# A gated recurrence on one core: a new order of TensorE's work in its loop, and new places for three of its products in PSUM

## The chip, the cores and the metric

The kernel runs as one program on one core of a Trainium2 chip. The metric is the device time of an execution in microseconds (us). One more execution was taken by the hardware profiler; all rows below are from it. The engines are TensorE (PE in the rows, PEld for its weight loads), VectorE (DVE), ScalarE (ACT), GpSimd (POOL) and SyncE, which only issues DMAs (SP). Matrix products are written to PSUM, which has eight banks; PE writes there, DVE and ACT read there, and POOL does not.

## The reference, cut to what matters

```python
B, H, S, D = 4, 8, 768, 48
state = np.zeros((B, H, D, D))
for t in range(S):
    kt, vt, rt = k[:, :, t], v[:, :, t], r[:, :, t]
    cur = einsum('bhd,bhe->bhde', u[None] * kt, vt)          # the bonus
    y[:, :, t] = einsum('bhd,bhde->bhe', rt, state + cur)
    state = w[None, :, :, None] * state + einsum('bhd,bhe->bhde', kt, vt)
x = y as rows of tokens, 3072 x 384
x = moe(x)      # skip score, 8 experts, one for each token; w1 is 384 x 1024, w2 is 1024 x 384
return moe2(x)  # 32 soft slots, again 8 experts
```

The change touches the first part alone, the recurrence.

## The kernel before

The recurrence is cut into 24 tiles: tile j = 4c + b is chunk c (128 time steps, six chunks) of batch b, with all eight heads. The eight heads lie as four pairs, one head of a pair in partitions 0 to 47 and one in 64 to 111. Within a chunk the sum over earlier steps is a masked product, and across chunks the state is carried. For each tile the kernel does this:

- `prep` (DVE, lines 614 and 615): r and k times powers of the decay, into `rks`; on POOL the product `pd` = r times k (617), and `prepk` (POOL, 623) the keys `kt` scaled for the state.
- `scores` (PE): eight products `sc` of keys and queries (632), into two banks of their own, then four small products `dt` (635), the bonus of each step, into bank t. ACT copies `dt` to SBUF as `dts` (637).
- `upd` (PE, 654): eight products of `kt` and the values, the chunk's addition to the state, into columns 160 to 351 of the bank named ud; `moved` (ACT, 670) copies it to `us`. For tiles 20 to 23 there is no update.
- `bonus` (PE, 657): one transpose of `dts`, into columns 0 to 127 of the same bank ud, under the name `dtk`.
- `amask` (DVE): the scores times a mask (681, `past`), then a predicated copy that puts `dtk` on the diagonal (688). The result is `at`.
- `inter` (PE, 708): eight products of the state and `rs`, which open y's two banks; from chunk 1 on. In chunk 0 three warm-up products stand in its place (493).
- `av` (PE, 718): eight products of the values and `at`, added in y's banks; ACT copies them to `yt` (721).
- `trx` (PE, 727): four transposes of `yt`, into bank t; ACT copies them to `x` (728).
- `decayed` and `state` (POOL, 664 and 676): the state times the decay of a chunk, plus `us`.

Beside that the router of the first mixture of experts is worked off, a chunk at a time: `route1` (PE, 750, four products of 512 columns, copied by ACT at 751), `route2` (PE, 810, four transposes), `route2b` (DVE, 826 to 843), `route3` (PE, 853 to 862), `gates`, `places` and `count` (DVE, 867 to 894), `route4` (POOL 908, DVE 909), and `scat` (POOL, 897), an indirect DMA that sends the rows of one tile to their expert.

All five engines are scheduled by hand: each one works its instructions off in the order in which the program writes them. So the order of calls in the loop over i sets everything. Loop i of the recurrence does, on PE: `scores(i)`, `upd(i)`, `bonus(i)`, `route3` and `route1` where they fall, `inter(i-1)`, `trx(i-2)`, `av(i-1)`, and `route2`. From i = 5 on the router has a turn of four loops: `route1` and `route2` in the first (i = 6, 10, 14, 18), `route2b` in the second, `route3`, `gates`, `places` and `count` in the third, `route4` in the fourth. Waits between engines are placed by the framework, by the tiles that instructions share: who writes a PSUM tile waits until the others that use it are done with it. Bank t, bank ud and the pair of y exist once, and so does the pair of `sc`. `rks` has three buffers; `pd`, `kt`, `us`, `tmp`, `at` and `dts` have two.

After the loops comes a short stretch that ends the routing, and then the experts, some 200 us, with nothing of the recurrence in it. The weights of the first expert are loaded from loops 20 to 22 on (`wload`).

Of the kernel before, what the change touches and what calls it, by code (L numbers as in the profile page):

```python
# [8 lines left out]
F32 = mybir.dt.float32  # L9
# [10 lines left out]
P = 128  # L20
# [3 lines left out]
E = 8  # L24
# [442 lines left out]
def tile_main(ctx, tc, rk, kv, wu, wcat, phi, w1, w2, v1, v2, r_in, k_in, v_in, w_in, u_in, wcn, out, dbg=None, force=False):  # L467
# [157 lines left out]
    def scores(j):  # L625
        t = T[j]
        ks, rs = t["ks"], t["rs"]
        sc = t["sc"] = psc.tile([P, 2, 4, P], F32, tag="sc", name=f"sc{j}")
        for p in range(4):
            for hf in range(2):  # L630
                r0 = 64 * hf
                nc.tensor.matmul(sc[:, hf, p, :], ks[r0 : r0 + D, p, :], rs[r0 : r0 + D, p, :], start=True, stop=True)  # L632
        dt_ = ps.tile([P, P], F32, tag="t", name=f"dt{j}")
        for p in range(4):
            nc.tensor.matmul(dt_[32 * p : 32 * p + 32, :], usel[:, p, :], t["pd"][:, p, :], start=True, stop=True)
        t["dts"] = wk.tile([P, P], F32, tag="dts", name=f"dts{j}")
        nc.scalar.copy(t["dts"], dt_)

    def newud(j):
        t = T[j]  # L640
        t["ud"] = ps.tile([P, 352], F32, tag="ud", name=f"ud{j}")
        t["dk"] = t["ud"][:, 0 : P + 4 * E]
        t["dtk"] = t["ud"][:, 0:P]

    def upd(j):
        t = T[j]
        if j < NT - B:
            kt, kvt = t["kt"], t["kv"]
            up = t["up"] = t["ud"][0:PR, 160:352].rearrange("d (p e) -> d p e", p=4)
            for p in range(4):  # L650
                for g in range(2):
                    h = head(p, g)
                    m = 64 if g == 0 else D
                    nc.tensor.matmul(up[64 * g : 64 * g + m, p, :], kt[:, h * D : h * D + m], kvt[:, 1, h * D : h * D + D], start=True, stop=True)

    def bonus(j):
        nc.tensor.transpose(T[j]["dtk"], T[j]["dts"], ident)  # L657
# [8 lines left out]
    def moved(j):  # L666
        t = T[j]
        if j < NT - B:
            t["us"] = sp[j][1] if j < B else wk.tile([PR, 4, D], F32, tag="us", name=f"us{j}")
            nc.scalar.copy(t["us"], t["up"])  # L670

    def state(j):
        t = T[j]
        c, b = divmod(j, B)
        if 0 < c and j < NT - B:
            nc.gpsimd.tensor_add(sp[b][(c + 1) % 2], t["us"], t["tmp"])
# [46 lines left out]
    def trx(j, tag="t", pool=ps):  # L723
        c, b = divmod(j, B)
        trp = pool.tile([P, 4, P], F32, tag=tag, name=f"trp{j}")
        for p in range(4):
            nc.tensor.transpose(trp[:, p, 0:PR], yts[c][:, p, b, :], ident[:PR, :PR])
        nc.scalar.copy(
            x[:, j, 0:DM].rearrange("t (p f d) -> t p f d", p=4, f=2),
            trp.rearrange("t p (f d) -> t p f d", d=64)[:, :, :, 0:D],  # L730
        )
        del T[j]
# [241 lines left out]
    if True:  # L974
        for i in range(NT):
# [7 lines left out]
                    r0 = 64 * hf  # L983
                    nc.vector.tensor_copy(usel[r0 : r0 + D, :, hf : hf + 1], wt[r0 : r0 + D, 1, :].rearrange("p (a o) -> p a o", o=1))
            scores(i)
            newud(i)
            if i > 0:
                upd(i)
                moved(i)
            bonus(i)  # L990
            if rok and (rb == 3 or i == 23):
                route3(rc, place=T[i]["dk"][:, P:])
            if rok and rb == 1 and rc < 4:
                route1(rc)
            if i > 0:
                inter(i - 1)
            if i > 1:
                trx(i - 2)
            if i == 0:
                decays()  # L1000
                warm(ps, "y", 7)
                prep(1)
                prepk(0)
                prepk(1)
                for ts in spf:
                    for t in ts:
                        nc.gpsimd.memset(t[:, 4 * D :], 0.0)
                upd(0)
                moved(0)
            elif i + 1 < NT:  # L1010
                prep(i + 1)
                prepk(i + 1)
            if i == 22:
                route2(4)
                mrt = rows(nc, cn, "t", rt, pa, "u", mcs[:, 0:1])
            amask(i)
            if i == 22:
                nc.vector.tensor_copy(lx[:, 0:1, :], mrt)
            decayed(i)
            state(i)  # L1020
            if i > 0:
                av(i - 1)
            if i == 21:
                route4(3)
                route1(4)
                nc.vector.tensor_reduce(cmax, ltm[:, 0:16, :].rearrange("t b s -> t s b"), axis=AX.X, op=ALU.max)
                colmax(nc, cn, "t", pa, "u", mcs[:, 0:1], fourfold(nc, "t", rt, cmax))
            elif rb == 0 and 1 <= rc < 4:
                route4(rc - 1)
            if rok and rb == 1 and rc < 4:  # L1030
                route2(rc)
            if i == 22:
                route2b(4)
            if rok and rb == 2 and rc < 4:
                route2b(rc)
            if i == 23:
                route1(5)
# [9 lines left out]
            if rok and rb == 3:  # L1047
                weave("gpgpgp", g=gates(rc), p=places(rc))
                count(rc)
            if 20 <= i < 23:  # L1050
                wload(i - 20)
            if 2 <= i < 6:
# [500 lines left out]
```

## Time and profile before

| | us |
|---|---|
| median of 3 runs | 372.65 |
| lowest, highest | 371.74, 373.26 |
| the profiled execution | 372.8 |
| its span, first to last instruction | 370.6 |
| busy in the span: PE, DVE, ACT, POOL | 339.3, 246.9, 149.7, 122.6 |

The span is 2.2 us shorter than the profiled execution's own time. The recurrence's first score product starts 8.22 us into the span, and the last loop's at 135.58. A busy PE in these tables is modelled from when matmuls start, so the distance from one group's start to the next tells more than its busy time.

### The profile page before, as it was taken

How to read it: one execution, taken by the hardware profiler on the slowest of the kernel's cores; microseconds unless marked ns; L12 is line 12 of the kernel's file. 1: busy time of each engine (PE TensorE's matmuls, PEld its weight loads, DVE VectorE, ACT ScalarE, POOL GpSimd, SP SyncE). 2: the span in 40 equal slices, each digit the busy share in tenths (PEclk: the TensorE clock that was granted, in tenths of full speed). 3: DMA queues.
4: the chain of work that ended last, by engine and by line, in shares of the span. 5: the costliest groups of instructions: out<-in, count | busy, mean ns of one | idle time of the engine just before them, and what ended most of it. 6: DMA issues, size and time to landing. Idle time of an engine off the chain costs nothing. (4 is left out here: it accounts for less than half of the span.)

```text
span 370.6 us, 8677 instructions
## 1 busy us (share of the span) xinstructions
PE 339.3 (92%) x3473; PEld 269.9 (73%) x3473; DVE 246.9 (67%) x502; ACT 149.7 (40%) x319; POOL 122.6 (33%) x165
## 2 busy tenths in 40 slices
PE   8899988989889887999999999999999999999860
PEld 3566665766756566489999999999899999734350
DVE  5788588595877985766567574848566856426660
ACT  1233332433333223445464555554655553311270
POOL 3765567686885605420020211202020202020000
PEclk9999999999999998799999999999999999999995
DMA  7999956455564961199968788778876457849485
GB/s 207 247 276 331 286 176 186 126 196 156 168 204 134 356 221 44 50 308 330 321 234 292 263 255 287 258 235 261 301 249 210 138 206 217 297 154 399 178 312 205
DMA packets 45743, 85.93 MB, mean 232 GB/s; under 512 B 3625, under 2 KB 26495, under 8 KB 45696
## 3 DMA queue, kind: packets, MB, share of 16 engines
q1 hardware_dynamic: 42368, 79.87, 66.6%
q0 software_dynamic: 2800, 5.28, 4.6%
q8 instruction: 29, 0.48, 0.5%
q10 hardware_dynamic: 528, 0.16, 0.2%
q14 instruction: 18, 0.15, 0.1%
HBM read 74.51 MB, written 13.30 MB: 237 GB/s over the span
## 5 line engine op out<-in xcount | busy, mean ns | idle before, releaser
L1155 PE MATMUL hp<-xhl,wa 128*128 128x256 f32 x192 | 48.6, 290 | 0.2 <-ACT xhl L1145 0.2
L1156 PE MATMUL hp<-xhl,wa 128*128 128x256 f32 x192 | 47.2, 282 | 0.0
L1180 PE MATMUL yp<-wb,hh 128*128 128x384 f32 x128 | 45.3, 354 | 0.0
L955 DVE TENSOR_TENSOR wa<-w,wa 128x768 fp32r<-128x768 f32 x32 | 30.5, 954 | 22.1 <-ACT wa L967 22.1
L1213 POOL DMA_INDIRECT lt_d<-lsr,id x16 | 17.6, 1097 | 80.2 <-ACT xhl L1145 56.7
L1181 PE MATMUL yp<-wb,hh 128*128 128x384 f32 x128 | 43.1, 337 | 0.0
L1182 PE MATMUL yp<-wb,hlo 128*128 128x384 f32 x128 | 43.1, 337 | 0.0
L688 DVE COPY_PREDICATED at<-ident,ud 128x1024 f32<-128x1024 int32 x24 | 31.6, 1318 | 8.1 <-PE ud L657 5.4
L1155 PEld LDWEIGHTS hp<-xhl,wa 128*128 128x128 f32 x192 | 36.4, 189 | 0.5 <-ACT xhl L1145 0.5
L1156 PEld LDWEIGHTS hp<-xhl,wa 128*128 128x128 f32 x192 | 36.5, 190 | 0.0
L681 DVE TENSOR_TENSOR at<-sc,mask 128x1024 f32<-128x1024 f32 x24 | 29.3, 1219 | 10.2 <-PE sc L632 10.2
L617 POOL TENSOR_TENSOR pd<-rkb 112x512 f32<-112x512 f32 x24 | 30.8, 1284 | 9.4 <-DMA rkb<-in_rk_dram 6.8
L955 DVE TENSOR_TENSOR wb<-w,wb 128x768 fp32r<-128x768 f32 x32 | 30.5, 954 | 3.2 <-ACT wb L967 3.2
L897 POOL DMA_INDIRECT xs_d<-x,idx x24 | 24.3, 1011 | 21.2 <-DVE idx L883 10.2
L967 ACT CAST wb<-w 128x768 fp32r<-128x768 f32 x32 | 26.8, 838 | 9.0 <-PE yp L1182 5.1
L1166 DVE SCALAR_TENSOR_TENSOR hlo<-hp,hh 128x512 fp32r<-128x512 f32 x32 | 22.0, 688 | 12.4 <-ACT hh L1165 12.4
L1165 ACT ACTIVATE hh<-hp 128x512 fp32r<-128x512 f32 x32 | 19.1, 598 | 26.2 <-PE hp L1158 25.9
L1158 PE MATMUL hp<-xhl,wa 128*128 128x256 f32 x192 | 28.3, 283 | 0.0
L632 PE MATMUL sc<-rks 48*128 48x128 f32 x384 | 27.9, 285 | 0.0
L967 ACT CAST wa<-w 128x768 fp32r<-128x768 f32 x32 | 26.9, 840 | 0.0
L1180 PEld LDWEIGHTS yp<-wb,hh 128*128 128x128 f32 x128 | 24.1, 188 | 3.5 <-issue 3.5
L632 PEld LDWEIGHTS sc<-rks 48*128 48x128 f32 x384 | 23.3, 187 | 4.4 <-issue 2.3
(327 smaller groups left out, 663.2 us busy)
## 6 DMA issues: line engine op xcount, KB each, us to landing
w<-in_w_dram SPq DMA_DIRECT2D x32, 768.0 KB
v<-in_v_dram SPq DMA_DIRECT2D x29, 768.0 KB
rkb<-in_rk_dram SPq DMA_DIRECT2D x24, 448.0 KB
kvt<-in_kv_dram SPq DMA_DIRECT2D x24, 384.0 KB
out_dram<-ob SPq DMA_DIRECT2D x5, 768.0 KB
xs_d<-zt SPq DMA_DIRECT2D x4, 774.0 KB
xg<-xs_d POOLq DMA_DIRECT2D x6, 387.0 KB, 6.5
x<-in_v_dram SPq DMA_DIRECT2D x2, 768.0 KB
```

The source lines that it names most:

```text
L617: nc.gpsimd.tensor_mul(t["pd"], rkt[:, 0], rkt[:, 1])
L632: nc.tensor.matmul(sc[:, hf, p, :], ks[r0 : r0 + D, p, :], rs[r0 : r0 + D, p, :], start=True, stop=True)
L681: nc.vector.tensor_mul(at, t["sc"], mask.rearrange("s (a o t) -> s a o t", a=1, o=1).to_broadcast([P, 2, 4, P]))
L688: nc.vector.copy_predicated(at, ident_i.rearrange("s (a o t) -> s a o t", a=1, o=1).to_broadcast([P, 2, 4, P]), t["dtk"].rearrange("s (p o ...
L955: nc.vector.tensor_sub(lv, sl, hv.bitcast(F32))
L967: nc.scalar.copy(hv, sl)
L1155: nc.tensor.matmul(hp[:, f, :], hi[:, k, fs], xh[:, k, :], start=(k == 0 and f == 0), stop=False)
L1156: nc.tensor.matmul(hp[:, f, :], lo[:, k, fs], xh[:, k, :], start=False, stop=False)
L1158: nc.tensor.matmul(hp[:, f, :], hi[:, k, fs], xl[:, k, :], start=False, stop=(k == 2 and f == 1))
L1180: nc.tensor.matmul(YP[e][bl], hh[:, f, bs], hi[:, f, :], start=st, stop=False)
L1181: nc.tensor.matmul(YP[e][bl], hh[:, f, bs], lo[:, f, :], start=False, stop=False)
L1182: nc.tensor.matmul(YP[e][bl], hlo[:, f, bs], hi[:, f, :], start=False, stop=en)
```

## The change

The bonus products `dt`, their transpose `dtk` and the router's `rp` now lie in one bank, ud, in this order. The update of the state goes to columns 256 to 447 of the second of y's two banks, beside the sums of tile i-1; from the second chunk on it no longer carries the flag that starts an accumulation, since `inter` has opened the bank. `trx(i-2)` moves up between `scores` and `bonus`, `route2` moves a loop later and stands behind `bonus`, `route1` stands behind `inter`, and `upd(i)` behind it, just ahead of `av(i-1)`. ACT's copy of the update follows the copy of y, and POOL's `state` is a loop later, ahead of `decayed`. The router's last `route4(3)` moves from loop 21 to loop 20.

```diff
--- before.py
+++ after.py
@@ -630,28 +630,24 @@
             for hf in range(2):
                 r0 = 64 * hf
                 nc.tensor.matmul(sc[:, hf, p, :], ks[r0 : r0 + D, p, :], rs[r0 : r0 + D, p, :], start=True, stop=True)
-        dt_ = ps.tile([P, P], F32, tag="t", name=f"dt{j}")
+        ud = ps.tile([P, 2 * P + 4 * E], F32, tag="ud", name=f"ud{j}")
+        dt_, t["dtk"], t["rp"] = ud[:, 0:P], ud[:, P : 2 * P], ud[:, 2 * P :]
         for p in range(4):
             nc.tensor.matmul(dt_[32 * p : 32 * p + 32, :], usel[:, p, :], t["pd"][:, p, :], start=True, stop=True)
         t["dts"] = wk.tile([P, P], F32, tag="dts", name=f"dts{j}")
         nc.scalar.copy(t["dts"], dt_)
 
-    def newud(j):
-        t = T[j]
-        t["ud"] = ps.tile([P, 352], F32, tag="ud", name=f"ud{j}")
-        t["dk"] = t["ud"][:, 0 : P + 4 * E]
-        t["dtk"] = t["ud"][:, 0:P]
-
     def upd(j):
         t = T[j]
         if j < NT - B:
             kt, kvt = t["kt"], t["kv"]
-            up = t["up"] = t["ud"][0:PR, 160:352].rearrange("d (p e) -> d p e", p=4)
+            yp = T[j - 1]["yp"] if j else ps.tile([PR, 2, 4 * P], F32, tag="y", name="yp")
+            up = t["up"] = yp[:, 1, 2 * P : 2 * P + 4 * D].rearrange("d (p e) -> d p e", p=4)
             for p in range(4):
                 for g in range(2):
                     h = head(p, g)
                     m = 64 if g == 0 else D
-                    nc.tensor.matmul(up[64 * g : 64 * g + m, p, :], kt[:, h * D : h * D + m], kvt[:, 1, h * D : h * D + D], start=True, stop=True)
+                    nc.tensor.matmul(up[64 * g : 64 * g + m, p, :], kt[:, h * D : h * D + m], kvt[:, 1, h * D : h * D + D], start=(j <= B), stop=(j <= B))
 
     def bonus(j):
         nc.tensor.transpose(T[j]["dtk"], T[j]["dts"], ident)
@@ -983,19 +979,17 @@
                     r0 = 64 * hf
                     nc.vector.tensor_copy(usel[r0 : r0 + D, :, hf : hf + 1], wt[r0 : r0 + D, 1, :].rearrange("p (a o) -> p a o", o=1))
             scores(i)
-            newud(i)
-            if i > 0:
-                upd(i)
-                moved(i)
+            if i > 1:
+                trx(i - 2)
             bonus(i)
             if rok and (rb == 3 or i == 23):
-                route3(rc, place=T[i]["dk"][:, P:])
+                route3(rc, place=T[i]["rp"])
+            if rok and (rb == 2 and rc < 4 or i == 22):
+                route2(rc)
+            if i > 0:
+                inter(i - 1)
             if rok and rb == 1 and rc < 4:
                 route1(rc)
-            if i > 0:
-                inter(i - 1)
-            if i > 1:
-                trx(i - 2)
             if i == 0:
                 decays()
                 warm(ps, "y", 7)
@@ -1005,33 +999,28 @@
                 for ts in spf:
                     for t in ts:
                         nc.gpsimd.memset(t[:, 4 * D :], 0.0)
-                upd(0)
-                moved(0)
             elif i + 1 < NT:
                 prep(i + 1)
                 prepk(i + 1)
+            if i > 0:
+                state(i - 1)
             if i == 22:
-                route2(4)
                 mrt = rows(nc, cn, "t", rt, pa, "u", mcs[:, 0:1])
+            upd(i)
+            if i > 0:
+                av(i - 1)
+            moved(i)
             amask(i)
+            decayed(i)
             if i == 22:
                 nc.vector.tensor_copy(lx[:, 0:1, :], mrt)
-            decayed(i)
-            state(i)
-            if i > 0:
-                av(i - 1)
             if i == 21:
-                route4(3)
                 route1(4)
                 nc.vector.tensor_reduce(cmax, ltm[:, 0:16, :].rearrange("t b s -> t s b"), axis=AX.X, op=ALU.max)
                 colmax(nc, cn, "t", pa, "u", mcs[:, 0:1], fourfold(nc, "t", rt, cmax))
             elif rb == 0 and 1 <= rc < 4:
                 route4(rc - 1)
-            if rok and rb == 1 and rc < 4:
-                route2(rc)
-            if i == 22:
-                route2b(4)
-            if rok and rb == 2 and rc < 4:
+            if rok and (rb == 2 and rc < 4 or i == 22):
                 route2b(rc)
             if i == 23:
                 route1(5)
@@ -1047,6 +1036,8 @@
             if rok and rb == 3:
                 weave("gpgpgp", g=gates(rc), p=places(rc))
                 count(rc)
+                if rc == 3:
+                    route4(3)
             if 20 <= i < 23:
                 wload(i - 20)
             if 2 <= i < 6:
```

PE in loop 9, before: `sc`, `dt`, the eight products of the update into `ud_858`, the transpose of the bonus, the state's product into y (`yp`), the four transposes of `yt` and the products with the values.

```order
L632 MATMUL sc_842<-rks_808 128x128 x8
L635 MATMUL dt_851<-pd_811,usel 32x128 x4
L654 MATMUL ud_858<-kvt_594,kt_813 64x48
L654 MATMUL ud_858<-kvt_594,kt_813 48x48
...
L657 MATMUL ud_858<-ident,dts_856 128x128
L708 MATMUL yp_870<-rks_721,sp_183 64x128
L708 MATMUL yp_870<-rks_721,sp_183 48x128 x2
...
L727 MATMUL trp_879<-ident,yt_588 128x112 x4
L718 MATMUL yp_870<-at_815,kvt_522 48x128 x8
L632 MATMUL sc_916<-rks_885 128x128 x8
```

PE in the same loop, changed (`trp` and `ud` are now the transposes and the bank of the bonus, `yp` takes the update as well):

```order
L632 MATMUL sc_833<-rks_789 128x128 x8
L636 MATMUL ud_842<-pd_792,usel 32x128 x4
L723 MATMUL trp_849<-ident,yt_575 128x112 x4
L653 MATMUL ud_842<-ident,dts_847 128x128
L704 MATMUL yp_856<-rks_703,sp_183 64x128
L704 MATMUL yp_856<-rks_703,sp_183 48x128 x2
...
L650 MATMUL yp_856<-kvt_588,kt_794 64x48
L650 MATMUL yp_856<-kvt_588,kt_794 48x48
...
L714 MATMUL yp_856<-at_816,kvt_517 48x128 x8
L632 MATMUL sc_906<-rks_865 128x128 x8
```

The transposes of `yt` have moved between `dt` and the bonus' transpose, and the update from there to just ahead of the products with the values.

ACT from loop 9's first copy to the next loop's, before: the bonus (`dts`), the update (`us`), the rows `x`, and `yt`.

```order
L637 COPY dts_856<-dt_851 128x128
L670 COPY us_867<-ud_858 112x192
L728 COPY x<-trp_879 128x384
L721 COPY yt_906<-yp_870 112x4x128
L637 COPY dts_930<-dt_925 128x128
```

The same stretch of ACT, changed:

```order
L638 COPY dts_847<-ud_842 128x128
L724 COPY x<-trp_849 128x384
L717 COPY yt_889<-yp_856 112x4x128
L666 COPY us_891<-yp_856 112x192
L638 COPY dts_920<-ud_915 128x128
```

The copy of the update has gone from behind the bonus' copy to behind that of `yt`, so it stands ahead of the next loop's bonus copy.

POOL in loop 9, before: `pd` and `kt` for tile 10, the decayed state `tmp` and the new state `sp` of tile 9, the router's copy and the indirect DMA.

```order
L617 TENSOR_TENSOR pd_888<-rkb_106 112x512
L623 TENSOR_TENSOR kt_890<-kvt_676,pktok 128x384
L664 TENSOR_TENSOR tmp_895<-sp_185,pt 112x192
L676 TENSOR_TENSOR sp_186<-us_867,tmp_895 112x192
L908 COPY ltt<-lg_673 128x128
L897 DMA xs_d<-x,idx 2048x387
```

POOL in loop 9, changed:

```order
L617 TENSOR_TENSOR pd_868<-rkb_106 112x512
L623 TENSOR_TENSOR kt_870<-kvt_662,pktok 128x384
L672 TENSOR_TENSOR sp_184<-us_814,tmp_819 112x192
L660 TENSOR_TENSOR tmp_896<-sp_185,pt 112x192
L904 COPY ltt<-lg_692 128x128
L893 DMA xs_d<-x,idx 2048x387
```

The new state that POOL adds up here is now tile 8's, whose update was copied at the end of the loop before.

## Rows read from the trace of the kernel before

**Rows 1.** The page's busy tenths of PE in 40 slices of the span:

```profile
PE   8899988989889887999999999999999999999860
```

**Rows 2.** Busy time by stretch (start:end, length, engines, PEclk, DMA share, GB/s):

```profile
60.27:83.14 22.87, 20.65 (x328) 14.92 (x326) 17.62 (x34) 7.62 (x19) 17.66 (x22) 1.00 0.57 168
...
143.00:146.00 3.00, 1.70 (x28) 1.22 (x24) 1.78 (x12) 0.54 (x3) 1.97 (x2) 1.00 0.24 83
146.00:149.00 3.00, 2.22 (x18) 2.22 (x19) 1.56 (x15) 1.16 (x3) 1.03 (x2) 0.51 0.07 25
160.00:340.00 180.00, 179.94 (x1340) 162.15 (x1341) 110.01 (x206) 89.05 (x172) 25.87 (x33) 1.00 0.77 259
```

**Rows 3.** Timeline of loop 9, PE and ACT (start, us, engine, line, operation, idle before):

```profile
55.28 1.16 PE L632 MATMUL sc<-rks 48*128 48x128 f32 x16
...
56.37 0.43 PE L635 MATMUL dt<-pd,usel 112*32 112x128 f32 x8
...
56.73 0.67 PE L654 MATMUL ud<-kvt,kt 128*64 128x48 f32 x16
56.92 0.27 ACT L637 COPY dts<-dt 128x128 f32<-128x128 f32 x1 [0.94 <-PE dt L635]
...
57.50 0.32 ACT L670 COPY us<-ud 112x192 f32<-112x192 f32 x1 [0.31 <-PE ud L654]
...
57.87 0.33 PE L657 MATMUL ud<-ident,dts 128*128 128x128 f32 x1 [0.48 <-ACT us L670]
...
58.13 0.67 PE L708 MATMUL yp<-rks,sp 48*64 48x128 f32 x16
...
58.73 0.60 PE L727 MATMUL trp<-ident,yt 112*128 112x112 f32 x4
...
59.26 1.08 PE L718 MATMUL yp<-at,kvt 128*48 128x128 f32 x16
...
60.27 1.16 PE L632 MATMUL sc<-rks 48*128 48x128 f32 x16
```

**Rows 4.** Timeline of PE in loop 20, which has no update:

```profile
119.25 0.43 PE L635 MATMUL dt<-pd,usel 112*32 112x128 f32 x8
120.12 0.33 PE L657 MATMUL ud<-ident,dts 128*128 128x128 f32 x1 [0.44 <-ACT dts L637]
```

**Rows 5.** Timeline of PE in loops 0, 1 and 2:

```profile
12.62 0.67 PE L654 MATMUL ud<-kvt,kt 128*64 128x48 f32 x16 [0.26 <-POOL kt L623]
13.21 1.16 PE L632 MATMUL sc<-rks 48*128 48x128 f32 x16
...
16.34 0.81 PE L493 MATMUL wp<-ones 128*128 128x512 bf16 x3
17.21 1.09 PE L718 MATMUL yp<-at,kvt 128*64 128x128 f32 x16
...
19.32 0.43 PE L635 MATMUL dt<-pd,usel 112*32 112x128 f32 x8
...
20.76 0.33 PE L657 MATMUL ud<-ident,dts 128*128 128x128 f32 x1 [0.43 <-ACT sp L670]
20.93 0.81 PE L493 MATMUL wp<-ones 128*128 128x512 bf16 x3
21.57 0.55 PE L727 MATMUL trp<-ident,yt 112*128 112x112 f32 x4
22.05 1.09 PE L718 MATMUL yp<-at,kvt 128*64 128x128 f32 x16
```

**Rows 6.** Waits from 20 to 140 us (waiting engine, line, releaser: us in total, times, longest):

```profile
PE ud L657 <- ACT us L670: 7.9, 16, 0.8
...
PEld trp L727 <- issue: 3.3, 19, 0.2
...
PE lgt L750 <- DVE ltt L909: 1.0, 1, 1.0
```

**Rows 7.** The costliest group of DVE from 20 to 140 us (busy us, mean ns, idle before):

```profile
L688 DVE COPY_PREDICATED at<-ident,ud 128x1024 f32<-128x1024 int32 x22 | 29.0, 1318 | 6.8 <-PE ud L657 5.4
```

## The prediction

> **What bounds the kernel now.** I read four views, from far to near. The busy slices of the page [rows 1] show TensorE at 0.8 to 0.9 of its time in the first 15 slices, which are the recurrence, a dip, and then 0.9 or more until the last two. The table by stretches says what that means. In the experts, from 160 to 340 us, PE is busy 179.94 of 180 us at a granted clock of 1.00, which is the level of 2.4 GHz [rows 2]. So nothing there waits for anything but PE, and whatever the recurrence gives back should move the whole rest forward. In the recurrence, one turn of four loops (10 to 13, 60.27 to 83.14) lasts 22.87 us, and no engine fills it: PE 20.65, DVE 17.62, POOL 17.66, ACT 7.62 [rows 2].
>
> Where PE's rest goes is read from the timeline of loop 9 [rows 3], which has none of the router's work on PE. By starts, the 4.99 us from one `sc` to the next are: `sc` 1.09, `dt` 0.36, `upd` 1.14, the bonus' transpose 0.26, `inter` 0.60, `trx` 0.53, `av` 1.01. One of them is too long. The update's products hold PE for 0.59 us where nothing stops the next group, in loop 0 (12.62 to 13.21 [rows 5]). Here the next group starts 1.14 us after them, and its row names the cause: idle 0.48, released by ACT's copy `us`. The transpose does not read `us`. It reads `dts`, whose copy ended at 57.19, 0.68 us before PE started; but update and transpose share bank ud, so PE waits until ACT has read the update out (57.82). The table of waits adds it up: 16 such waits, 7.9 us in all, none over 0.8 [rows 6]. That is the wait which ends last in every loop with an update, and it stands on the engine that sets the pace.
>
> **The change, part by part.** All sums are against the profiled execution, 372.8 us (span 370.6 and 2.2 around it); it lies 0.15 above the median of 372.65, which I neglect.
>
> *The bonus no longer waits for the update.* The update goes to y's bank and behind `inter`, so the transpose waits for `dts` alone. How long that takes is seen in loop 20, where there is no update: from `dt` to the transpose 0.87 us, 0.44 of it idle for `dts` [rows 4]. In loop 9 it is 57.87 - 56.37 = 1.50 us [rows 3].
>
> *`trx` moves into the gap that is left.* From `dt` PE is held 0.36 us, then `trx` 0.53 [rows 3]: 0.89 us, just what the copy of the bonus needs (0.87). So the transposes cost nothing where they stand now, and the bonus starts 0.89 after `dt`. Their cover is the wait for `dts`; without it they would cost their 0.53 again.
>
> *The update is paid where it stands.* Ahead of `av` it costs its own 0.59 [rows 5]. It waits for `kt`, which POOL makes a loop earlier.
>
> A plain loop then takes 1.09 + 0.89 + 0.26 + 0.60 + 0.59 + 1.01 = 4.44 us in place of 4.99: 0.55 less. There are 15 such loops, 5 to 19; what the router adds on PE in them is the same before and after. 15 x 0.55 = **8.3 us**.
>
> *Loops 1 to 4*, with warm-up products in place of `inter`. In loop 2 from `dt` to `av` 22.05 - 19.32 = 2.73 us. After: 0.87 to the bonus (`trx` is shorter here, 0.48, so the wait for `dts` decides), 0.17 to the warm-up, then the update must wait until the warm-up, which writes the same bank, is through, 0.87 as `av` does in loop 1 (16.34 to 17.21), and 0.59: 2.50 [rows 4, 5]. 0.23 less, four times: **0.9 us**.
>
> *Loops 20 to 23* have no update, and the wait for `dts` is there already. `trx` moves into it: 4 x 0.53 = **2.1 us** [rows 3, 4].
>
> *`route4(3)` a loop earlier.* In loop 21 PE waits 1.0 us for DVE's line 909 before `route1` [rows 6]. That wait goes, but the transpose behind `route1` needs a reduction on DVE that starts no earlier than its predicated copy ends, so something else is late next. Between 0 and 1.0 I take **0.3 us**, nearer to nothing, since DVE gains no time of its own.
>
> *Edits at no cost.* `route2` behind the bonus and `route1` behind `inter` bring the same products to other places; what they read is copied in the loop before. ACT now has `yt` and `us` ahead of the next `dts`: 0.59 and 0.32 us, over about 1.0 us into the loop, while `dt` is ready only at 1.64 (56.92 - 55.28 [rows 3]). If POOL were late with `state`, `us` would wait for its buffer, `dts` behind it, and PE behind that; but POOL's 17.66 us of work in a turn stand against some 20.6 that PE will need, and `state` now has a loop's time. `dt` now shares its bank with `dtk` and `rp`, so `dt(i)` waits until DVE's predicated copy of the loop before is done. In a plain loop the bonus starts 1.98 us after `sc`, the copy follows some 0.4 later and takes 1.32 [rows 7], ending near 3.7; the next `dt` comes at 4.44 + 1.09 = 5.5. That is 1.8 us of cover. The earlier loads follow the earlier `av`; POOL and DVE had been waiting for PE, not for them.
>
> A rule bears on these new neighbours in a bank. The Trainium skill (PSUM — Partial Sum Buffer, Terms) says that two engines must not be on the same bank and partitions at once. The 0.48 us of loop 9 agree: PE waited for ACT though the two used different columns of ud. The rule speaks against putting `dt` beside `dtk`, since one wait between PE and a reader of the bank goes and another comes; by it alone the sum would depend on the 1.8 us of cover, and the first rival below is that case.
>
> **Sum:** 8.3 + 0.9 + 2.1 + 0.3 = 11.6 us. 372.8 - 11.6 = **361.2 us**. I leave uncounted that loop 10 waits 0.8 in place of 0.48 [rows 6].
>
> **The rivals.**
>
> *The predicated copy becomes late.* DVE has 17.62 us of work in a turn and PE will need about 20.7 (22.87 less four times 0.55), so DVE has 3 us left; but it can use them only in the loop with `route1`, where it must wait for scores. In the three others it works almost without a break, and a lag there reaches PE at `dt` or at `sc`. For it: DVE takes over 0.8 of a shortened turn. Against it: the cover of 1.8 us, and two buffers of `at`. Taken at 1 us a turn, over half of that cover, it costs 5 us in five turns: **366 us**.
>
> *The new seams cost.* PE's weight loads stand idle by 0.17 us ahead of `trx` where it follows `inter`, 19 times, 3.3 us, with no releaser [rows 6]. My sum has such a gap behind `dt` and behind `inter` (they are in the 0.36 and 0.60), none between `trx` and the bonus, or between update and `av`. One such gap in 19 loops is 3.3 us, 364.5; both are 6.6, **368 us**. Against it: before the change `trx` passes to `av` in 0.53 us, a little less than its modelled 0.60 [rows 3], so not every seam has one.
> The Trainium skill (TensorEngine Tiling (Array Packing), Key Properties) says that changing the tiling mode drains the engine. By that rule the new pairs, whole-array transposes side by side and two groups on the same columns, pay nothing, and this rival falls; the rows agree only in part, because `trx` to `av` changes the mode too and shows no gap.
>
> *The gain does not reach the end.* The experts could begin when weights or gathered rows land. Then the time stays **372.8**. For it: that stretch also hangs on DMAs. Against it: the first weights are issued in loops 20 to 22, which move along, and the DMA share is 0.24 just after the loops [rows 2].
>
> *Slower: the clock.* After a stretch in which PE was busy 1.70 of 3.00 us the granted clock fell to 0.51, the level of 1.2 GHz [rows 2], and PE's work takes about twice its time there. Five to nine transposes now stand in a row in each loop. If the clock fell because of them, a turn's 20 us of work would take some 20 us more. It decides from about 12 us of work at the lower level on; one whole turn gives 361 + 20 = **381 us**. Against it: PE idles less than before, and it was granted 1.00 in a turn with 90% busy [rows 2].
>
> **How the numbers follow.** The forecast gets 0.78, spread over 358.5 to 363.5: the ends are 0.05 a loop either way on the seams (1 us), the 0.7 left of the 1.0 in loop 21, and some 1.5 us that the stretch at the lower clock behind the loops may gain or lose by where it falls. The late copy gets 0.06, the seams 0.09, no gain 0.03, the clock 0.04. A range from 358.5 to 366.0 takes in the forecast, a late copy, and the half of the seams' case with one gap; it leaves out no gain, the clock and the other half, and a tail of the forecast, together under 0.2. Half a per cent, about what can be told from no change, is 1.9 us. Faster is 0.78 + 0.06 + 0.09 = 0.93, of which I give 0.01 back; same 0.04, slower 0.04.
>
> **What would show it.** In the changed profile a plain loop should take about 4.4 us from `sc` to `sc`; the bonus' transpose should start 0.85 to 0.95 after `dt`, with next to no idle; `us` should release nothing on PE; the update should hold PE about 0.6; a turn should last near 20.7, and the last loop's `sc` start near 124.5 instead of 135.58. A wait of `dt` for DVE's line of the predicated copy would show the first rival, idle weight loads ahead of the bonus or of `av` the second, and a granted clock below 1.00 before 130 us the last. I am wrong if a turn is over 21.5, or if the recurrence ends 11 us earlier and the kernel does not.

## The result

The changed kernel took 358.58 us (median of 4 runs, 356.83 to 361.48), the kernel before beside it 372.95: a ratio of 0.962, 95% interval 0.955 to 0.970. Two later comparisons on other chips gave 0.960 (0.956 to 0.964) and 0.957 (0.951 to 0.963). So the change is worth 14 to 16 us; 361.2 was forecast, with a range from 358.5 to 366.0, and the median lies 0.08 us above its lower end.

The profiled execution is the longest of the four: 361.48, span 359.7. The four fall into two groups by their mean granted clock, 356.8 and 357.7 us at 0.978, 359.5 and 361.5 at 0.968 and 0.965, and the profiled one is in the second.

### The profile after

The page's busy tenths of PE and its granted clock, in 40 slices, against [rows 1]:

```profile
PE   8899999999998978999999999999999999999850
...
PEclk9999999999999995899999999999999999999985
```

Busy time by stretch, in the columns of [rows 2]: the turn of loops 10 to 13, four stretches behind the loops, the experts.

```profile
55.36:75.10 19.74, 19.53 (x327) 14.65 (x326) 17.61 (x34) 7.12 (x19) 18.50 (x23) 1.00 0.79 221
129.00:131.00 2.00, 0.86 (x12) 0.57 (x12) 0.96 (x9) 0.25 (x2) 1.70 (x2) 1.00 0.29 102
131.00:133.00 2.00, 0.57 (x5) 0.57 (x6) 1.04 (x11) 1.07 (x3) 0.02 (x1) 1.00 0.15 56
133.00:135.00 2.00, 1.81 (x28) 1.71 (x27) 1.58 (x12) 0.45 (x2) 1.38 (x2) 0.60 0.07 28
135.00:147.00 12.00, 11.10 (x67) 3.31 (x66) 7.38 (x20) 4.14 (x9) 3.55 (x5) 0.50 0.41 124
150.00:330.00 180.00, 180.00 (x1346) 161.79 (x1348) 109.39 (x203) 88.55 (x169) 24.59 (x32) 1.00 0.75 255
```

The turn went from 22.87 us with PE busy 20.65 to 19.74 with 19.53: PE is nearly full now. The experts run as before. Between loops and experts is a stretch at the lower level, 1.2 GHz: about 1.6 us of 133 to 135 (mean 0.60) and 12 us to 147, 13.7 us by the granted clock of the trace. Before it PE had been busy 1.43 of 4 us. In the kernel before, such a stretch came to 6.8 us.

Loop 9 on PE and ACT, against [rows 3]:

```profile
51.07 1.16 PE L632 MATMUL sc<-rks 48*128 48x128 f32 x16
52.16 0.43 PE L636 MATMUL ud<-pd,usel 112*32 112x128 f32 x8
52.52 0.60 PE L723 MATMUL trp<-ident,yt 112*128 112x112 f32 x4
53.03 0.33 PE L653 MATMUL ud<-ident,dts 128*128 128x128 f32 x1
53.29 0.67 PE L704 MATMUL yp<-rks,sp 48*64 48x128 f32 x16
53.89 0.61 PE L650 MATMUL yp<-kvt,kt 128*64 128x48 f32 x15
54.29 0.30 PE L714 MATMUL yp<-at,kvt 128*48 128x128 f32 x1
54.33 0.22 PE L650 MATMUL yp<-kvt,kt 128*64 128x48 f32 x1
54.39 1.04 PE L714 MATMUL yp<-at,kvt 128*48 128x128 f32 x15
...
51.67 0.32 ACT L666 COPY us<-yp 112x192 f32<-112x192 f32 x1
52.71 0.27 ACT L638 COPY dts<-ud 128x128 f32<-128x128 f32 x1 [0.71 <-PE ud L636]
```

4.29 us to the next `sc` at 55.36, in place of 4.99, and no idle time ahead of any product. The bonus' transpose (L653) starts 0.87 after `dt`, behind the transposes. The first product of the values (54.29) stands ahead of the last one of the update (54.33): the two groups run into each other and take 1.47 us together.

The table of waits from 18 to 124 us, against [rows 6], which listed 7.9 us of PE for `us`:

```profile
POOL pd L617 <- DMA rkb<-in_rk_dram: 8.3, 5, 2.6
...
PEld yp L650 <- issue: 5.6, 20, 0.6
PEld trp L723 <- issue: 4.2, 21, 0.2
...
PE c4pt L94 <- DVE c4t L88: 1.6, 1, 1.6
...
PE ud L653 <- ACT dts L638: 0.2, 1, 0.2
```

The wait for `us` is gone, and in this window the table names two waits of PE for another engine: 1.6 us in loop 21, and 0.2 in loop 11.

| from `sc` to `sc`, us | before | after | gain | forecast |
|---|---|---|---|---|
| loops 1 to 4 | 19.55 | 17.93 | 1.62 | 0.9 |
| loops 5 to 19 | 85.40 | 73.66 | 11.74 | 8.3 |
| loops 20 to 22 | 17.42 | 16.00 | 1.42 | 1.9 |
| `sc` of loop 23 to the first expert product | 24.48 | 27.42 | -2.94 | 0.5, spread 1.5 |

In a second profiled execution the loops were the same to 0.02 us (17.93, 73.66, 16.01), and the last line was 24.41. So the recurrence gives 14.8 us in both, and the stretch behind it decides whether some of that is given back.

### The profile page after: what moved, and what is told of

Its sections match the earlier page's. It is cut to its first block, busy times and chain, and to the rows that moved or that the text cites. A ratio compares the mean times of both kernels' runs of the same rounds, so it can differ in the third digit from the quotient of the medians.

```text
span 359.7 us, 8663 instructions
## 1 busy us (share of the span) xinstructions
PE 337.2 (94%) x3473; PEld 268.3 (75%) x3473; DVE 246.2 (68%) x502; ACT 148.0 (41%) x319; POOL 122.5 (34%) x165
## 5 line engine op out<-in xcount | busy, mean ns | idle before, releaser
L717 ACT COPY yt<-yp 112x512 f32<-112x512 f32 x24 | 14.0, 585 | 41.4 <-PE yp L714 38.9
L714 PE MATMUL yp<-at,kvt 128*48 128x128 f32 (+1 forms) x384 | 26.9, 275 | 0.0
```

## The experiments

Twelve runs followed: the changed kernel twice and ten variants. Loops are measured from the traces; the time of a whole run also has the stretch behind the loops in it, so each is compared with kernels of its own chip.

### The changed kernel again

> The changed kernel once more, for a second trace and for the comparisons of this chip. If the stretch behind the loops explains the spread of its runs (356.8 to 361.5), runs at a mean granted clock near 0.978 last 356 to 358 and runs near 0.966 some 3 us more; the loops themselves repeat within 0.2 us (loops 5 to 19 in 73.7). If the spread comes from the loops, their length moves with the time instead.

Measured 357.83 us (before there: 373.34): 356.9 to 358.1 at a granted clock of 0.978, and 360.0 at 0.969, as expected; loops 5 to 19 took 73.67. On a third chip:

> The changed kernel on another chip, for the comparisons of this call. Where the kernel before has its stretch at the lower clock behind the loops (its clock near 0.978), the ratio is again 0.957 to 0.964; where it has none (its time near 369.4, clock 0.985), the recurrence's 14 to 15 us are all there is, 354.5 to 356, ratio 0.960 to 0.963.

358.83 us (before: 374.01), a ratio of 0.957. The stretch from the last `sc` to the first expert product, profiled in both (the first repeat, then the second):

```profile
120.42:144.83 24.41, 21.11 (x235) 13.17 (x233) 16.54 (x74) 10.16 (x25) 10.06 (x12) 0.86 0.25 79
```

```profile
121.09:148.39 27.30, 23.61 (x235) 13.22 (x233) 16.76 (x74) 10.06 (x25) 10.03 (x12) 0.75 0.32 100
```

The same 235 products at a mean clock of 0.86 and of 0.75. Time at the lower level is twice what is missing to 1.00: 6.8 us (2 x 0.14 x 24.41) in the first, 13.7 in the second. The loops were equal. Of the 3.4 us between the two spans (355.9 and 359.3) 2.9 come from here, beside 6.8 us more at the lower level, and 0.7 from a later start of the recurrence.

### The update away from the values

```diff
+            if i > B:
+                T[i - 1]["yp"] = ps.tile([PR, 2, 4 * P], F32, tag="y", ...)
+                upd(i)
             if i > 0:
                 inter(i - 1)
...
-            upd(i)
+            if i <= B:
+                upd(i)
             if i > 0:
                 av(i - 1)
```

> The changed kernel with the update's products (loops 5 to 19) back ahead of inter, in the same bank, so that they no longer stand next to the values' products. Theory: update and values run into each other and take 1.47 us together where they take 0.59 + 1.01 apart, so each of 15 loops loses 0.13 us, a plain loop goes from 4.29 to 4.42 and the kernel is 2.0 us slower than the changed one. Rival: the place of the update is indifferent, what counted was only the wait that went; then a plain loop stays at 4.29 and the time does not move. A second rival: a gap appears on each side of the update, 0.17 each, and the loop takes 4.6 to 4.75, 5 to 7 us slower.

The update's products now open their columns themselves, with the starting flag in every chunk. A plain loop took 4.42 us, the others of loops 5 to 19 were 0.12 to 0.16 longer too: 75.72 in place of 73.66. The whole took 361.33. Its profiled execution, at a clock of 0.979, has 1.4 us more of span than that of the changed kernel at 0.978 on this chip (357.2 to 355.9); its loop 21, 0.13 shorter, and its earlier start, 0.45, hide the rest of the 2.1. PE in one of its plain loops:

```profile
52.53 0.67 PE L650 MATMUL yp<-kvt,kt 128*64 128x48 f32 x16
53.13 0.67 PE L706 MATMUL yp<-rks,sp 48*64 48x128 f32 x16
53.72 1.08 PE L716 MATMUL yp<-at,kvt 128*48 128x128 f32 x16
54.73 1.16 PE L632 MATMUL sc<-rks 48*128 48x128 f32 x16
```

Update 0.60, `inter` 0.59, values 1.01, without a gap, and without the overlap of update and values. The theory's 0.13 holds; both rivals fall.

### The transposes back behind inter

```diff
             scores(i)
-            if i > 1:
-                trx(i - 2)
             bonus(i)
...
+            if i > 1:
+                trx(i - 2)
             if i == 0:
                 decays()
```

> The changed kernel with the transposes back behind inter (and route1), all else as changed. Theory: the transposes are free only while they stand in the wait for dts; behind inter they cost their 0.53 again and 0.44 of waiting comes back behind dt, of which the 0.36 of dt were not part: the bonus 0.87 after dt, a plain loop 1.09 + 0.87 + 0.26 + 0.60 + 0.53 + 1.47 = 4.82 us, 0.53 more in 22 loops, 10 to 12 us slower than the changed kernel, so 369 to 370. Rival: the gain came from the update's new bank alone, since the wait for us went with it; then a plain loop stays near 4.3 to 4.4 and the time within 2 us of the changed kernel.

368.08 us, 10.25 more than the changed kernel on that chip; a plain loop 4.82, loops 5 to 19 82.24.

```profile
55.30 0.33 PE L653 MATMUL ud<-ident,dts 128*128 128x128 f32 x1 [0.44 <-ACT dts L638]
...
56.16 0.60 PE L723 MATMUL trp<-ident,yt 112*128 112x112 f32 x4
56.69 0.61 PE L650 MATMUL yp<-kvt,kt 128*64 128x48 f32 x15
```

With nothing to do behind `dt`, PE waits its 0.44 for `dts`, and the transposes cost 0.53 where they stand. Without the transposes in the wait, the new places are worth only 0.17 in a plain loop (4.99 to 4.82), of which 0.13 is update and values side by side: one wait is traded for another.

### The transposes in the old wait

The kernel before, with one edit:

```diff
                 upd(i)
                 moved(i)
+            if i > 1:
+                trx(i - 2)
             bonus(i)
...
                 inter(i - 1)
-            if i > 1:
-                trx(i - 2)
```

> The kernel before with one edit: the transposes stand between the update and the bonus' transpose, where PE waits 0.48 us for us; the update stays in the bank of the bonus. Theory: what matters is that the transposes stand in a wait, not which wait: a plain loop takes 1.09 + 0.36 + 0.59 + 0.53 + 0.26 + 0.60 + 1.01 = 4.44 us, or 4.55 if 0.1 of the wait for us is left; loops 20 to 23 gain nothing, since dt and the transposes share a bank and these wait 0.44 for dts first. 15 loops by 0.44 to 0.55 and some 0.2 in loops 2 to 4: 7 to 9 us faster than before, 364 to 366, and the changed kernel beats it by what loops 20 to 23 (2 us), and update and values side by side (2 us) give. Rival: without the new bank for the update nothing is gained, the wait for us only moves: 372 to 374.

364.61 us, a ratio of 0.979 (0.973 to 0.984) to before; a plain loop 4.46, loops 5 to 19 77.41.

```profile
53.76 0.67 PE L654 MATMUL ud<-kvt,kt 128*64 128x48 f32 x16
54.36 0.60 PE L727 MATMUL trp<-ident,yt 112*128 112x112 f32 x4
54.91 0.33 PE L657 MATMUL ud<-ident,dts 128*128 128x128 f32 x1
```

The update still shares its bank with the transpose, and no idle time is left ahead of it. Either wait, for `us` or for `dts`, is filled by 0.53 us of transposes. The new bank adds 0.17 a loop to that (4.29), 0.13 of it the overlap of update and values; and it lets the transposes run into the wait in loops 20 to 23 as well, where this kernel gained nothing (loops 20 to 22 took 17.74, against 17.42 before and 16.00 after: here `dt` and the transposes share a bank).

### The router's products in their old places

```diff
-            if rok and (rb == 2 and rc < 4 or i == 22):
+            if i == 22:
                 route2(rc)
+            if rok and rb == 1 and rc < 4:
+                route1(rc)
             if i > 0:
                 inter(i - 1)
...
+            if rok and rb == 1 and rc < 4:
+                route2(rc)
...
             if i == 21:
+                route4(3)
                 route1(4)
```

> The changed kernel with the router's products in their old places (route1 ahead of inter, route2 at the end of the same loop, route4(3) in loop 21). Theory: these moves were worth 0.15 us for each of route1 and route2, four times each in loops 5 to 19, so 73.66 becomes 74.9 us, and about 0.15 in loop 21; 358.9 to 359.6. If the saving came from what the other edits leave around them, loops 5 to 19 stay at 73.7. A cost over 2 us would mean that route2, right behind route1 in one loop, waits for ACT's copy of the scores.

Loops 5 to 19 took 75.80, more than the 74.9 expected. `route1` and `route2` cost 1.87 and 0.58 as before (1.72 and 0.43 in the changed kernel): that part, 4 x 0.31, is as expected. The rest is new: in three of the four loops with `route1` (10, 14 and 18), PE now waits ahead of `dt`. Waits of PE from 18 to 118 us, and the rows at `dt` of loop 14:

```profile
PE lgt L746 <- DVE ltt L905: 2.1, 1, 2.1
PE ud L636 <- DVE at L684: 0.7, 2, 0.3
PE ud L636 <- POOL kt L623: 0.3, 1, 0.3
PE ud L636 <- DVE lgp L865: 0.3, 1, 0.3
```

```profile
75.22 1.32 DVE L684 COPY_PREDICATED at<-ident,ud 128x1024 f32<-128x1024 int32 x1
...
76.68 0.43 PE L636 MATMUL ud<-pd,usel 112*32 112x128 f32 x8 [0.35 <-POOL kt L623]
```

The last row names POOL, but `kt` is not read by `dt`; what ends 0.14 ahead of it (75.22 + 1.32) is the predicated copy of loop 13, which reads the bank that `dt` of loop 14 writes. In loops 10 and 18 the copy itself is named (the 0.7 above). By the length of the loops it is 0.41 us each. That is the first rival of the prediction, at a price of 1.2 us (0.3 came back in loop 11). The wait for L865 is in loop 21 and of another kind; the next experiment shows it larger. `route4(3)` in loop 21 costs a wait of 2.1 us ahead of `route1`, where the changed kernel has 1.6 behind it; loop 21 took 9.02, some of it at the lower level, so I don't read its price off. The whole was 359.64 (before on that chip: 369.37).

### More work for DVE

```diff
             amask(i)
+            if 5 <= i < 20:
+                nc.vector.tensor_copy(kp_extra, ident)
             decayed(i)
```

> The changed kernel with one more copy on DVE in each of loops 5 to 19, 128 x 128 values right behind the predicated copy, some 0.25 us, whose result nobody reads. In the changed kernel dt of the loops with route1 starts only 0.17, 0.37 and 0.16 us after the predicated copy of the loop before has ended (loops 10, 14, 18), though it is 1.74 in loops 3 to 5. Theory: DVE falls behind through the three loops without route1 and is at its limit there, so four extra copies a turn (1.0 us) show as a wait of dt for the predicated copy in loops 10, 14 and 18, 0.6 to 0.9 us each, and loops 5 to 19 take 75.5 to 76.5 in place of 73.66, the kernel 2 to 3 us more than the changed one at the same clock. Rival: DVE has 2.1 us free in a turn of 19.74 (17.61 busy) and takes them: loops 5 to 19 stay at 73.7.

The extra copies took longer than I thought, 0.20 to 1.90 us (the last section has two of them). DVE's busy time in loops 10 to 13 rose from 17.61 to 20.61: 3.0 us where 2.1 were free (19.74 - 17.61), so 0.9 was the least that this turn had to lose. It lost 1.64 (21.38). Loops 14 to 17 lost 2.09 (21.54 against 19.45), with 2.8 more where 2.2 were free. So DVE's free time is not all to be had, as the theory said, though the load was not the 1.0 us a turn that it named. Loops 5 to 19 took 77.77, 4.1 us more; the whole 359.75 (before on that chip: 368.87).

Plain loops 13 and 17 went from 4.29 to 5.31, the first two (5 and 9) stayed at 4.28 and 4.29: the lag builds up over the turns. The waits stand only in part where they were expected: `dt` waited for the predicated copy by 0.18, 0.34 and 0.34 us in loops 10, 14 and 18, and by 0.85 and 0.84 in loops 13 and 17, where the releaser is another:

```profile
72.30 0.17 DVE L875 TENSOR_TENSOR r<-ud,oh 128x32 f32<-128x32 f32 x1
72.42 0.17 DVE L866 TENSOR_SCALAR lgp<-lgp 128x4 f32<-128x4 f32 x1
...
72.62 0.43 PE L637 MATMUL ud<-pd,usel 112*32 112x128 f32 x8 [0.85 <-DVE lgp L866]
```

L866 does not touch the bank. The row above it does: `r` reads the router's `rp` of loop 12 there, behind the predicated copy, and ends 0.15 ahead of `dt`, as the copy does where it is the releaser. So the bank has a second late reader on DVE, in the loops with `route3`, and that one was the dearer here. The prediction priced the first alone.

### The column maxima later

```diff
             scores(i)
+            if i == 22:
+                colmax(nc, cn, "t", Banks(u=[(ps, "r", 1)]), "u", mcs[:, 0:1], c4)
...
-                colmax(nc, cn, "t", pa, "u", mcs[:, 0:1], fourfold(nc, "t", rt, cmax))
+                c4 = fourfold(nc, "t", rt, cmax)
```

> The changed kernel with one more move, of the transpose of the column maxima from the end of loop 21 to behind the dt products of loop 22 (in the router's bank). In loop 21 of the changed kernel PE waits 1.6 us for DVE's c4t ahead of that transpose, and sc of loop 22 stands behind it. Theory: the wait is all that route4(3) left of its saving; sc of loop 22 then starts some 1.8 us earlier, of which 0.25 come back for the transpose in loop 22: 1.3 to 1.6 us faster than the changed kernel. Rival: DVE, which has the reduction, the two products and the predicated copy behind each other there, sets the pace of loops 21 and 22, and the wait reappears at sc of loop 23: under 0.3 us.

Loop 21 took 5.55 in place of 7.44, loop 22 5.08 in place of 4.59: 1.41 us less over loops 20 to 22 (14.59). The whole was 355.55, a ratio of 0.961 (0.958 to 0.965) to before on its chip. There is no run of the changed kernel on that chip, so only the loops are compared. Behind them PE met a wait for gathered rows, just ahead of the first expert product:

```profile
140.64 0.97 PE L1136 MATMUL xtp<-ident,xg 128*128 128x128 f32 x6 [2.04 <-DMA xg<-xs_d]
```

In the two other variants on that chip without products of ones this wait was 0.63 us, and no other trace has it. So where results come in time the landing of the rows is the next bound, and the 1.41 need not all reach the end.

### Products of ones behind the loops

```diff
         av(23)
+        fill(psc.tile([P, 2, 4, P], F32, tag="sc", name="fl")[:, 0, 0:3, :], 2)
         route3(5, "t", (4,))
...
         trx(22, "tp", pc)
+        fill(w1g.ps[:, 0 : 3 * P], 10)
         direct(7, "y")
```

> The changed kernel with twelve extra products of ones (384 columns, 0.16 us each by the rate of the warm-up's rows) behind the loops, where TensorE waits: two ahead of the last tiles' places, ten behind the transposes of tile 22; their results are overwritten. Nothing is left out. Theory: behind the loops the granted clock falls to its lower level because PE waits there, for 6.83 us in the quick runs and 13.65 us in the slow ones, and this is what makes the runs of the changed kernel differ by 3 to 5 us; with PE kept busy the stretch from the last loop's sc to the first expert's product goes from 24.4 us (27.4 in the slow run) to 21 to 22.5, the kernel to 354.5 to 356.5, and the spread falls under 1.5 us. Rival: the products only delay what follows or the clock falls all the same: 357.5 to 360, with the same two groups of runs.

356.07 us, from 355.06 to 357.11; the spread of 2.05 is more than the 1.5 of the theory.

> The same twelve products in the kernel before. Theory: its one stretch of 6.83 us at the lower level goes too, up to 3.4 us: 370 to 371.5; so the gain of the change is the same with and without the stretch, 15 to 16 us. Rival: the stretch is met by something else and the time stays at 373.

369.04 us against 369.37: no change, and a miss. The kernel before ran there at a clock of 0.984 to 0.988, against 0.978 where its trace has the stretch, so by its clock this chip had no such stretch to begin with, and nothing was learned of the cure. What the pair does show is the gain without the stretch: both profiles have a clock of 1.00 from the last `sc` to the experts (21.09 and 21.63 us), and their spans are 353.3 and 367.5, a difference of 14.2.

> The twelve products behind the loops once more, beside the changed kernel on the same chip. Theory: where the changed kernel has a stretch at the lower clock behind the loops, the products take most of it away, 2 to 4 us faster; where it has none, they cost up to 1 us, since ten of them outlast the wait for yt. Rival: no difference on a chip with the stretch.

358.85 us against 358.83 of the changed kernel on the same chip: no gain, and the theory falls. PE came to the ten products only after the standstill, and they ran at the lower level:

```profile
130.94 0.60 PE L727 MATMUL trp<-ident,yt 112*128 112x112 f32 x4 [1.91 <-remote]
131.38 3.24 PE L497 MATMUL dpst<-ones 128*128 128x384 bf16 x10
134.42 1.24 PE L770 MATMUL lgp<-wcs,yt 112*128 112x42 f32 x8
```

```profile
131.38:135.00 3.62, 3.62 (x16) 2.21 (x14) 0.95 (x10) 0.67 (x3) 1.94 (x2) 0.53 0.08 29
```

In this execution the time at the lower level was 3.4 us (2 x 0.47 x 3.62), half of the 6.8 of the first repeat. Yet its stretch to the experts took 25.44 us against 24.41 there: the ten products stood in the way, and the products with `wcs` behind them began at 134.42, in the first repeat at 131.57.

> The column maxima's transpose behind the dt products of loop 22, as in the experiment before, with six products of ones in place of twelve (two and four). Theory: the 1.4 us of loops 21 and 22 and what the products save or cost add up: 1.4 us faster than the changed kernel where there is no stretch at the lower clock, 3 to 5 us where there is one; 352.5 to 355. Rival: four products are too few, the stretch comes as without them and only the 1.4 us are left.

358.65 us, also no gain, though its runs lie closer together (357.95 to 359.07). Of the 1.4 us of loops 21 and 22 only 0.43 were there (5.55 and 6.06 against 7.45 and 4.59): ACT's copy of `dt` in loop 22 came late (last section), and PE waited 0.97 us for it. So the version with the later column maxima is better by its loops where PE's results come in time, and not shown better as a whole.

## Why the prediction was right, and where not

**The wait.** That the bonus waited for `us` by the shared bank, 0.48 in loop 9 and 7.9 in all, was right, and so was what replaces it: `dt` to bonus 0.87 measured, 0.89 forecast, `us` releasing nothing on PE, and `dts` once, 0.2 us.

**The plain loop** was mis-sized: 4.44 forecast, 4.29 measured. The step that failed is "Ahead of `av` it costs its own 0.59": update and values together take 1.47, not 0.59 + 1.01. The row of loop 0, from which the 0.59 came, has another kind of product behind the update. The experiment with the update away from the values puts a price on it: 0.13 a loop, 2.0 us; why this pair overlaps no run shows. The other 0.02 is from the transposes to the bonus, 0.51 in place of 0.53.

**"What the router adds on PE in them is the same before and after"** was wrong: `route1` costs 1.72 in place of 1.87 and `route2` 0.43 in place of 0.59, 0.31 a turn or 1.2 us in four. So 15 x 0.70 + 1.2 is the measured 11.74, in place of 8.3.

**Loops 1 to 4:** 1.62 in place of 0.9. Loops 2 to 4 gave 0.34 each (0.23 and most of the 0.13 above). Loop 1, which has no transposes to place, gave 0.58; I had taken it as another loop 2.

**Loops 20 to 22:** loop 20 gave 0.53, as forecast. Loop 21 gave 0.15, where 0.53 and 0.3 had been forecast: the wait of 1.0 went from ahead of `route1` to ahead of the transpose of the column maxima, 1.59 us for DVE's `c4t`. The text had named that place; "nearer to nothing" was not near enough. The later column maxima show that it held up `sc` of loop 22. Loop 22 gave 0.74.

**The end.** 361.2 was close to the profiled 361.5 by two errors of like size: the recurrence gave 14.8 in place of 11.1 up to the last `sc`, and 2.9 of it were lost to a second piece at the lower level behind the loops, where the text allowed 1.5. So the nearness is luck. The median of 358.6 has less of that loss, and the two executions with the higher clock, 356.8 and 357.7, lie under the range: the mechanism was right, its gain was forecast too small, and the lower clock hid part of that.

**The rivals.** *The predicated copy becomes late:* it did not, but by a hair. The prediction read its cover of 1.8 us from a plain loop with no lag, and it holds in loops 3 to 5 (1.74). Later in a turn DVE falls behind:

```profile
54.97 1.31 DVE L684 COPY_PREDICATED at<-ident,ud 128x1024 f32<-128x1024 int32 x1
...
56.45 0.43 PE L636 MATMUL ud<-pd,usel 112*32 112x128 f32 x8
```

0.17 us of cover are left for `dt` of loop 10 (56.45 - 54.97 - 1.31), 0.37 and 0.16 in loops 14 and 18, and 2.25 right behind a loop with `route1` (loop 19: 98.08 + 1.32 to 101.65). Where `dt` waited for the copy it began 0.14 behind its end, so 0.17 is next to nothing to spare. The old places of the router's products and the extra copy both made it a wait. The price in the prediction counted five turns; there are four loops with `route1`, and it came in three of them. The Trainium skill (PSUM — Partial Sum Buffer, Terms), by which two engines must not be on one bank and the same partitions at once, spoke against this neighbourhood; the waits of `dt` for the copy in those two kernels agree with it.

*The seams:* none of the gaps that were feared. The idle weight loads ahead of the transposes are as before (4.2 us in 21, against 3.3 in 19), those ahead of the update 5.6 us in 20, of which the first loops have the long ones behind the warm-up, and PE's products show no idle time there from loop 5 on (0.1 us in each of loops 1 to 4). The sign was the other way round: this pair side by side gains. *The gain does not reach the end:* it does, 14.2 us of span where the clock was equal; but the wait for gathered rows with the later column maxima shows that this rival is near. *The clock:* 1.00 up to 133 us, through all loops of the changed kernel, so the slower case did not come; what came is a longer stretch at the lower level behind the loops.

**"POOL and DVE had been waiting for PE, not for them"** no longer holds for DVE, by the covers above. For POOL the 8.3 us of waiting for loads of `rkb` belong to this execution: both repeats of the changed kernel have 1.5 there, and the kernel before 0.9. None of it reached PE.

**A row misread, without effect:** the busy slices of before [rows 1] end with three below 0.9 (8, 6, 0), not two.

## What to carry to other kernels

When the engine that sets the pace has a short wait in every loop, look first whether independent work can be moved into it: that reordering alone gave 0.53 of the 0.70 us of a plain loop here, and 8.7 of the 15.5 us of the whole. Price a moved group by the neighbours that it will have, not by the row where it stood: the update's products ran into the values' here, 0.13 us a loop that no row of before showed. And take a cover from the loop where the next engine is furthest behind, not from the plainest one, and from the last reader of the bank: 1.7 us in one loop were 0.2 in another, and more work on that engine cost time.

## What was not expected of the hardware

**Results that come late.** On the chips where the kernel before took 373 to 374 us, in it and in every version profiled, the copies that follow the last products of the recurrence begin 2.2 to 2.8 us behind the end of these products. The last values' products of before and ACT's copy of them:

```profile
142.74 1.08 PE L718 MATMUL yp<-at,kvt 128*48 128x128 f32 x16
...
146.14 0.59 ACT L721 COPY yt<-yp 112x512 f32<-112x512 f32 x1 [1.27 <-PE trp L727]
```

The same two in the version with the router's old places, on a chip where before took 369.4:

```profile
133.32 1.08 PE L714 MATMUL yp<-at,kvt 128*48 128x128 f32 x16
...
134.45 0.58 ACT L717 COPY yt<-yp 112x512 f32<-112x512 f32 x1 [0.68 <-PE yp L714]
```

2.32 us behind the end of the products in the one, 0.05 in the other; in the version with six products of ones `dt` of loop 22 ran from 115.79 to 116.22 and its copy began at 117.70. Where results came late (nine profiles), PE, ACT and DVE stood still together for a while, and the clock fell to its lower level between 0.05 us ahead of the late copy and 2.1 us behind it; where they came in time (five profiles, all on that other chip) it did not fall between the last `sc` and the experts. Which of the two is the cause of the other, or what third thing holds the results, no run here shows. It was in the kernel before as well, so the change neither made nor mended it.

**What the lower level costs.** 6.8 us more at 1.2 GHz went with 2.9 to 3.0 us more of the stretch (24.41 to 27.30 and 27.42), less than the half of 6.8; that part of it is spent waiting would explain it, but is not shown.

**A copy that ends with another engine's work.** The extra copies on DVE, all alike, took 0.20 to 0.22 us in five of the fifteen loops and 0.37 to 1.90 in the ten others. Each of the ten ended 0.08 to 0.10 us after an instruction of POOL that had overlapped it; the five met no POOL work beyond their first 0.02 us. One of the ten, in which POOL passed from `pd` to `kt`, and one of the five:

```profile
64.81 1.63 DVE L1016 COPY extra<-ident 128x128 f32<-128x128 f32 x1
65.34 1.00 POOL L624 TENSOR_TENSOR kt<-kvt,pktok 128x384 f32<-128x384 f32 x1
...
81.38 0.21 DVE L1016 COPY extra<-ident 128x128 f32<-128x128 f32 x1
```

By these ends the ten waited for POOL: all fifteen took 9.4 us, where 15 times the short 0.21 are 3.1. So the price of such a copy hangs on where it falls.
